# Row maxima by way of DRAM in 4-byte elements, in place of VectorE's transposition, in an attention block with a gated FFN

## The chip, the core and the metric

The kernel runs on one core of one Trainium2 chip. The metric is the device time of one execution in microseconds. The kernel before takes 1174.17 us (median of three runs, 1174.13 to 1174.26). Its engines are TensorE (PE, with its weight loads as PEld), VectorE (DVE), ScalarE (ACT), GpSimd (POOL) and SyncE (SP), which issues nearly all DMAs. Tiles lie in SBUF with 128 partitions; matmuls write to eight PSUM banks.

## What is computed

The reference is a pre-norm transformer block in float32 with one shared key and value head:

```
B, S, D, H, F = 1, 2048, 448, 16, 1792          # Dh = 28
q = (ln(x) @ wq) in 16 heads;  k = ln(x) @ wk;  v = ln(x) @ wv      # k, v: one head for all 16
p = softmax(q k^T * Dh ** -0.5)                                     # over 2048 keys
h = x + (p v, heads side by side) @ wo
out = h + (silu(ln(h) @ w1) * (ln(h) @ w3)) @ w2
```

## The kernel before

**Groups and steps.** The 2048 queries make four tiles of 512 (T), the 16 heads four sets of four. A group i, 0 to 15, is one tile of queries with four heads; head j of the group lies in partitions 32j to 32j + 27. Attention of a group runs over 16 steps, one for each 128 keys (`c`), so there are 256 steps. The loop takes them in pairs.

**Two passes over the scores.** The softmax subtracts each query's maximum before the exponential. The maxima of a group are found ahead, 20 steps before its heads: `Unit` multiplies 128 queries of one head with 512 keys into a PSUM bank (L277), and DVE takes the maximum over them into one column of MX (`red`, L283, or with a second half joined in, `both`, L291). The second pass (`Head`, L328) computes the scores the other way round, keys in the partitions and 512 queries along the row, as three matmuls of split high and low parts. ACT takes the exponential from PSUM (L338), and `pv` multiplies with the values (L346).

**How the maximum gets into the scores.** The 28 channels of a head leave four of its 32 partitions free. Partition 28 + 32j of the high plane of the group's query tile QS[i] holds the negated maximum of every query, and the key tile has a row of ones there. So the matmul of L328 subtracts the maximum. But `max_done` finds the maxima with queries in partitions: after L307, NEG[q, 4j + n] is the negated maximum of query 128n + q of head j. They have to get from 128 partitions with 16 columns into 4 partitions with 512 columns. Before, DVE's transposition of blocks of 32 x 32 (L308, into NGT) and four DMAs from SBUF to SBUF (`max_out`, L314), one for each 32 queries, do that.

**Order.** The order is written out by hand. ORDER gives, within a pair of steps, the place of each score unit (u, d, t), each head matmul (0a to 7c) and each `pv` (p). Everything else hangs on step numbers: `max_done(i)` at step 16i - 5 and `max_out(i)` at 16i - 4. Each is called at the end of its pair; the first head of group i comes early in the pair 16i. Instructions of an engine run in the order in which they are written, and each waits for its inputs. SP's instruction for a DMA takes its turn on SP, waits there, and then the transfer runs by itself; the DMAs have eight semaphores in rotation.

**Neighbours on SP.** Behind the maxima stand, in each group, four copies of the group before's softmax denominators (`sm<-OT`, L355), a write of their reciprocals to DRAM (`sd<-sm`, L363) and four reads that spread them over partitions (`rb<-sd`, L366). In group 2, gathers of queries (`QR<-QR`, L487 to L493) stand ahead of the maxima and behind them. Group 0's maxima are finished in a hand-written list (FRONT) ahead of the loop.

Of the kernel before, what the change touches and what calls it, by code (L numbers as in the profile page):

```python
# [8 lines left out]
F32 = mybir.dt.float32  # L9
# [13 lines left out]
T = 512  # L23
NT = S // T
NQ = T // P
# [25 lines left out]
def block_kernel(  # L51
# [13 lines left out]
    ve, se, ge, pe, sy = nc.vector, nc.scalar, nc.gpsimd, nc.tensor, nc.sync  # L65
# [4 lines left out]
    def f(ap):  # L70
        return ap.bitcast(F32)
# [6 lines left out]
    dr_pool = ctx.enter_context(tc.tile_pool(name="dr", bufs=2, space=DRAM))  # L78
# [5 lines left out]
    NEG = [keep.tile([P, 32], F32R, name="neg")] * 2  # L84
    NGT = [keep.tile([P, 32], F32, name=f"ngt{k}") for k in range(2)]
# [161 lines left out]
    QS, MX, PT, PO, WH, WS = {}, {}, {}, {}, {}, {}  # L247
# [56 lines left out]
    def max_done(i):  # L304

        neg = NEG[i % 2]
        ve.tensor_reduce(neg[:, :16], MX[i], axis=AX.X, op=ALU.max, negate=True)  # L307
        ve.transpose(NGT[i % 2], f(neg))  # L308

    def max_out(i):  # L310

        dst = f(QS[i][28::32, 0]).rearrange("j (n b x) -> j n b x", n=NQ, b=4)
        for b in range(4):
            sy.dma_start(dst[:, :, b], NGT[i % 2][32 * b : 32 * b + 16])  # L314
# [272 lines left out]
    def maxima(i):  # L587
        max_done(i)
        max_out(i)
# [29 lines left out]
    for i in range(1, NI):  # L619
        at(NC * i - 5, max_done, i)  # L620
        at(NC * i - 4, max_out, i)
# [218 lines left out]
```

## Time and profile before

| | before |
|---|---|
| median of the runs | 1174.17 us |
| the profiled execution | 1174.14 us |
| its span in the trace | 1172.0 us |
| attention with both passes | about 75 to 696 us of the span |
| FFN | from about 740 us to the end |
| PE, DVE, ACT, POOL busy | 99%, 69%, 62%, 29% |
| `max_done`: L307 and L308 | 16 times each, 0.22 and 0.21 us |
| `max_out`: L314 | 64 DMAs of 2 KB, on SP |

Times in the rows are us from the span's start. A timeline row gives start, length, engine, line, operation, tiles and shapes, how many were merged, and in brackets the idle time ahead and what ended it. A row of the windows gives the stretch, its length, the busy us of PE, PEld, DVE, ACT and POOL with their instructions, the granted share of TensorE's clock, the mean busy share of the 16 DMA engines and GB/s. A row of the waits gives who waited for whom, us in total, how often, and the longest.

### The profile page before, as it was taken

What the parts mean: (1) busy time and instruction counts of PE and PEld (TensorE: products, weight loads), DVE (VectorE), ACT (ScalarE), POOL (GpSimd) and SP (SyncE); (2) the same over time, 40 slices, a digit from 0 to 9 for tenths busy, and PEclk for the clock granted to TensorE, in tenths of its full rate; (3) what the DMA queues carried; (4) which work ended last, traced back from release to release, by engine and by line L of the source; (5) the groups of instructions that cost most, each with busy time, mean ns of one, the idle gap of its engine ahead of it and who ended that gap; (6) DMA issues with size and microseconds to landing.
All of it is one profiled execution on the core that took longest, in us unless ns stands there. A gap on an engine that the chain in (4) does not pass through costs nothing. (4 is left out here: it accounts for less than half of the span.)

```text
span 1172.0 us, 24130 instructions
## 1 busy us (share of the span) xinstructions
PE 1159.4 (99%) x9552; PEld 720.2 (61%) x9552; DVE 812.2 (69%) x1482; ACT 728.1 (62%) x1385; POOL 334.0 (29%) x275
## 2 busy tenths in 40 slices
PE   9999999999999999999999999999999999999998
PEld 7654444445444445444445443688888888888887
DVE  8879999997898997999987972364445445444443
ACT  5779999996899996999986999311211121111111
POOL 5202110110110111111011032364555445445552
PEclk9999999999999999999999999999999999999999
DMA  5110110000010000010000010113000000000000
GB/s 171 42 29 2 43 50 5 11 11 3 11 47 11 2 11 11 2 48 11 3 11 11 3 46 11 51 51 103 1 32 1 1 1 32 1 1 32 1 1 32
DMA packets 33158, 27.72 MB, mean 24 GB/s; under 512 B 11215, under 2 KB 29327, under 8 KB 33045
## 3 DMA queue, kind: packets, MB, share of 16 engines
q1 hardware_dynamic: 32484, 26.12, 7.6%
q8 instruction: 75, 1.23, 0.4%
q14 instruction: 39, 0.31, 0.1%
q10 hardware_dynamic: 560, 0.06, 0.0%
HBM read 20.25 MB, written 3.80 MB: 21 GB/s over the span
## 5 line engine op out<-in xcount | busy, mean ns | idle before, releaser
L338 ACT ACTIVATE pt<-pb 128x512 f32<-128x512 f32 x1024 | 531.7, 610 | 11.0 <-PE pb L328 5.2
L283 DVE TENSOR_REDUCE mx<-pa 128x1 f32<-128x512 f32 x708 | 460.9, 684 | 52.1 <-PE pb L328 36.9
L328 PE MATMUL pb<-qs,KH 32*128 32x512 f32 x2048 | 342.8, 431 | 0.1
L277 PE MATMUL pa<-KH,qs 32*128 32x512 f32 x866 | 327.4, 487 | 0.3
L346 PE MATMUL po<-pt,VA 128*32 128x256 f32 (+1 forms) x2984 | 298.1, 471 | 5.9 <-ACT OT L350 5.5
L328 PE MATMUL pb<-qs,KL 32*128 32x512 f32 x1024 | 283.2, 419 | 0.0
L328 PEld LDWEIGHTS pb<-qs,KH 32*128 32x128 f32 x2048 | 174.9, 182 | 114.1 <-DVE mx L283 50.0
L165 PE MATMUL pa<-xh,w 128*128 128x512 f32 x784 | 202.1, 391 | 0.0
L728 ACT ACTIVATE rb<-pa 128x512 f32<-128x512 f32 x56 | 30.4, 595 | 250.5 <-PE pa L720 250.4
L165 PEld LDWEIGHTS pa<-xh,w 128*128 128x128 f32 x784 | 146.1, 188 | 30.4 <-issue 1.2
L277 PEld LDWEIGHTS pa<-KH,qs 32*128 32x128 f32 x866 | 142.8, 181 | 9.5 <-issue 1.8
L328 PEld LDWEIGHTS pb<-qs,KL 32*128 32x128 f32 x1024 | 136.4, 182 | 2.4
L745 PE MATMUL pb<-w2s,hid 128*128 128x448 f32 x648 | 136.9, 366 | 0.0
L346 PEld LDWEIGHTS po<-pt,VA 128*32 128x32 f32 x2984 | 58.8, 108 | 122.7 <-issue 105.3
L745 PEld LDWEIGHTS pb<-w2s,hid 128*128 128x128 f32 x648 | 119.4, 188 | 17.3 <-issue 9.8
L287 ACT ACTIVATE relu<-pa 128x512 f32<-128x512 f32 x158 | 91.2, 600 | 58.7 <-PE pa L277 49.4
L392 POOL TENSOR_TENSOR w<-QR,w 128x1024 fp32r<-128x1024 f32 x32 | 84.0, 2641 | 94.2 <-PE pa L720 79.9
L291 DVE CUSTOM_DVE_ANT_0 relu<-pa,relu 128x512 f32<-128x512 f32 x158 | 105.5, 682 | 7.5 <-PE pa L277 4.1
L737 DVE TENSOR_TENSOR hid<-rb,hid 128x512 fp32r<-128x512 f32 x56 | 72.3, 1290 | 39.2 <-ACT hid L736 39.2
L370 POOL TENSOR_TENSOR OT<-OT,rb 128x512 f32<-128x512 f32 x16 | 20.5, 1284 | 273.5 <-ACT pt L338 147.0
L165 PE MATMUL pa<-xl,w 128*128 128x512 f32 x336 | 94.5, 389 | 0.0
L391 DVE CAST w<-QR 128x1024 fp32r<-128x1024 f32 x32 | 22.2, 695 | 89.5 <-PE pa L165 81.3
(125 smaller groups left out, 948.2 us busy)
## 6 DMA issues: line engine op xcount, KB each, us to landing
rb<-sd SPq DMA_DIRECT2D x64, 64.0 KB
QR<-in_B_w_dram SPq DMA_DIRECT2D x16, 192.0 KB
X<-in_A_x_dram SPq DMA_DIRECT2D x3, 896.0 KB
out_dram<-X SPq DMA_DIRECT2D x3, 896.0 KB
w<-in_B_w_dram SPq DMA_DIRECT2D x8, 192.0 KB
w_wo<-in_B_w_dram SPq DMA_DIRECT2D x6, 224.0 KB
qs<-ngt SPq DMA_DIRECT2D x64, 2.0 KB
sm<-OT SPq DMA_DIRECT2D x64, 2.0 KB
```

Of the source, the lines that this page charges most:

```text
L165: pe.matmul(ps, lhs[b][:, cb, lsl], rhs[a][:, ca, rsl], start=(k == 0), stop=(k == len(terms) - 1 and not part),)
L277: pe.matmul(self.ps, QS[i][r, 0, n * P : (n + 1) * P], ks[r], start=True, stop=True)
L283: ve.tensor_reduce(self.col(), self.ps, axis=AX.X, op=ALU.max)
L287: se.activation(r, self.ps, AF.Relu)
L291: ve.tensor_tensor_reduce(r, self.ps, r, 1.0, LOW, op0=ALU.add, op1=ALU.max, accum_out=self.col())
L328: pe.matmul(self.ps, (KH, KH, KL)[k][r, c * P : (c + 1) * P], QS[i][r, (0, 1, 0)[k]], start=(k == 0), stop=(k == 2))
L338: se.activation(pt, self.ps, AF.Exp, bias=0.0, scale=SCALE)
L346: pe.matmul(PO[i][32 * j : 32 * j + 32, q], VA[:, c], PT[i, c, j][:, q], start=(c == 0 and h0 == 0), stop=(c == NC - 1 and h1 == 2))
L392: ge.tensor_tensor(wl, W13[k], f(wh), op=ALU.subtract)
L728: se.activation(sg, ps[0], AF.Silu)
L737: ve.tensor_tensor(h[:, 1], sg, f(h[:, 0]), op=ALU.subtract)
L745: pe.matmul(Y[t][n][:, :D], hid[a][:, n * P : (n + 1) * P], w2s[:, b, :D], start=(k == 0 and m == 0), stop=(k == NF - 1 and m == 2))
```

## The change

For groups 1 to 15, `max_done` leaves the transposition out. `max_out` writes the 16 columns of NEG to a DRAM tile `mxd` of 4 x 512, where neighbouring columns of a partition lie 512 bytes apart and neighbouring partitions 4 bytes apart, so every run is one element of 4 bytes; there are 2048. A second DMA reads the four rows of 512 elements from DRAM into the four partitions of QS[i]. Group 0 keeps the transposition and the four DMAs.

```diff
         neg = NEG[i % 2]
         ve.tensor_reduce(neg[:, :16], MX[i], axis=AX.X, op=ALU.max, negate=True)
-        ve.transpose(NGT[i % 2], f(neg))
+        if i == 0:
+            ve.transpose(NGT[0], f(neg))
 
     def max_out(i):
 
+        if i > 0:
+            sd = dr_pool.tile([4, T], F32, name="mxd")
+            sy.dma_start(sd.rearrange("j (n q) -> q j n", n=NQ), f(NEG[i % 2][:, :16]).rearrange("q (j n) -> q j n", n=NQ))
+            sy.dma_start(f(QS[i][28::32, 0]), sd)
+            return
         dst = f(QS[i][28::32, 0]).rearrange("j (n b x) -> j n b x", n=NQ, b=4)
         for b in range(4):
             sy.dma_start(dst[:, :, b], NGT[i % 2][32 * b : 32 * b + 16])
```

The first place is DVE around the maxima of group 3, with what each instruction waits for. Before:

```order
L283 TENSOR_REDUCE mx_87<-pa 128x1 [waits PE_49] x6
L291 ISA relu,mx_87<-pa,relu 128x512 [waits PE_49]
L291 ISA mx_87 128x1
L307 TENSOR_REDUCE neg<-mx_87 128x16 [waits DVE_49]
L308 STREAM_TRANSPOSE ngt_84<-neg 128x32 [waits DMAHW2_49,DVE_49]
L283 TENSOR_REDUCE mx_86<-pa 128x1 [waits PE_49] x6
```

Now:

```order
L283 TENSOR_REDUCE mx_87<-pa 128x1 [waits PE_49] x6
L291 ISA relu,mx_87<-pa,relu 128x512 [waits PE_49]
L291 ISA mx_87 128x1
L307 TENSOR_REDUCE neg<-mx_87 128x16 [waits DMAHW0_49,DVE_49]
L283 TENSOR_REDUCE mx_86<-pa 128x1 [waits PE_49] x6
```

The transposition is gone, and the wait for the DMA of an earlier group that still may read the tile has moved from it to L307.

The second place is SP around the maxima of group 2, where gathers stand on both sides (the loop's L487 is L493 in the changed file). Before:

```order
L487 DMA QR_100<-QR_100 4x512 x2
L487 DMA QR_100<-QR_100 4x512 [waits DMAHW1_49]
L314 DMA qs<-ngt_83 4x4x32 [waits DVE_49,PE_49]
L314 DMA qs<-ngt_83 4x4x32
L314 DMA qs<-ngt_83 4x4x32 [waits DMAHW4_49]
L314 DMA qs<-ngt_83 4x4x32 [waits DMAHW5_49]
L487 DMA QR_100<-QR_100 4x512 [waits DMAHW6_49]
```

Now:

```order
L493 DMA QR_100<-QR_100 4x512 x2
L493 DMA QR_100<-QR_100 4x512 [waits DMAHW7_49]
L315 DMA mxd<-neg 128x16x1 [waits DVE_49]
L316 DMA qs<-mxd 4x512 [waits DMAHW0_49,PE_49]
L493 DMA QR_100<-QR_100 4x512 [waits DMAHW2_49]
```

Two DMAs stand in place of four, and the second waits on SP for the landing of the first (DMAHW0).

## The prediction

> **What bounds the kernel now.** I read the page first, then the windows of the attention stage, then VectorE's (DVE's) timeline around one place where the maxima of a group are finished, and last the DMA issues of SyncE.
>
> ```profile
> span 1172.0 us, 24130 instructions
> PE 1159.4 (99%) x9552; PEld 720.2 (61%) x9552; DVE 812.2 (69%) x1482; ACT 728.1 (62%) x1385; POOL 334.0 (29%) x275
> 317.00:400.00 83.00, 82.31 (x935) 37.80 (x932) 74.92 (x141) 78.72 (x152) 10.15 (x10) 1.00 0.08 21
> ```
>
> The 99% of PE tells little: matmul ends are modelled. In a stretch of pure attention (the third row: 83 us, then the busy us of PE, PEld, DVE, ACT, POOL) DVE is busy 90% and ACT 95%. PE, ACT and DVE run in lockstep, handing each other eight PSUM banks, so a delay on any of them that exceeds its slack lengthens the pair of steps in which it falls. The next fence is DVE's timeline. L291 runs once in each pair, so the distance between two L291 rows is a pair's length.
>
> ```profile
> 349.05 0.68 DVE L291 CUSTOM_DVE_ANT_0 relu<-pa,relu 128x512 f32<-128x512 f32 x1
> ...
> 353.93 0.68 DVE L291 CUSTOM_DVE_ANT_0 relu<-pa,relu 128x512 f32<-128x512 f32 x1
> 354.53 0.08 DVE L291 DVE_READ_ACCUMULATOR2_ANT mx<- 128x1 f32 x1
> 354.65 0.22 DVE L307 TENSOR_REDUCE neg<-mx 128x16 fp32r<-128x64 f32 x1
> 354.90 0.21 DVE L308 STREAM_TRANSPOSE ngt<-neg 128x32 f32<-128x32 f32 x1
> 355.04 3.12 DVE L283 TENSOR_REDUCE mx<-pa 128x1 f32<-128x512 f32 x5
> ...
> 359.15 0.68 DVE L291 CUSTOM_DVE_ANT_0 relu<-pa,relu 128x512 f32<-128x512 f32 x1
> ...
> 364.03 0.68 DVE L291 CUSTOM_DVE_ANT_0 relu<-pa,relu 128x512 f32<-128x512 f32 x1
> ...
> 374.42 0.68 DVE L291 CUSTOM_DVE_ANT_0 relu<-pa,relu 128x512 f32<-128x512 f32 x1
> ...
> 375.03 0.25 DVE L362 RECIPROCAL sm<-sm 128x16 f32<-128x16 f32 x1
> 375.19 1.82 DVE L283 TENSOR_REDUCE mx<-pa 128x1 f32<-128x512 f32 x3
> ...
> 379.30 0.68 DVE L291 CUSTOM_DVE_ANT_0 relu<-pa,relu 128x512 f32<-128x512 f32 x1
> ```
>
> An ordinary pair takes 353.93 - 349.05 = 4.88 us. The pair with the maxima takes 359.15 - 353.93 = 5.22, so 0.34 more, and the next is at 4.88 again. In an ordinary pair the reductions of L283 start with the accumulator read; here they start at 355.04 instead of 354.53, 0.51 late. The pair with the reciprocal has them only 375.19 - 375.03 = 0.16 late and takes 4.88: nothing lost. So DVE has between 0.16 and 0.51 us of slack in a pair, and what exceeds it is paid. The way it is paid shows on ScalarE:
>
> ```profile
> 356.94 3.21 ACT L338 ACTIVATE pt<-pb 128x512 f32<-128x512 f32 x6 [0.15 <-PE pb L328]
> PEld pb L328 <- DVE mx L283: 50.0, 123, 0.4
> ```
>
> The late reduction frees its bank late, PE starts the next scores late, and ACT waits 0.15 us for them in the middle of its exponentials.
>
> **The change, part by part.** First the transposition. It runs sixteen times, and fifteen of them go:
>
> ```profile
> L308 DVE STREAM_TRANSPOSE ngt<-neg x16: 211/211/213, 70.5 to 695.6; 128x32 f32<-128x32 f32 x16
> ```
>
> The fifteenth, at 695.6, has no reduction behind it (the score units are over), so removing it is worth nothing; fourteen count. What remains in front of the reductions is the reduction L307 and the gap before it. The transposition starts 0.25 after L307 (354.90 - 354.65), and that step goes out of the delay of 0.51: 0.26 remains. (A wait for the earlier copy of the maxima stands in front of L307 now; that copy is an entire group old, so only its few tens of ns could show.) What a delay of 0.26 costs is read from other rows. At the start of the attention DVE has casts at the same place:
>
> ```profile
> 93.81 0.68 DVE L291 CUSTOM_DVE_ANT_0 relu<-pa,relu 128x512 f32<-128x512 f32 x1
> ...
> 94.42 0.39 DVE L502 CAST WO<-OT 128x448 fp32r<-128x448 f32 x1
> 94.72 3.16 DVE L283 TENSOR_REDUCE mx<-pa 128x1 f32<-128x512 f32 x5
> ...
> 98.86 0.68 DVE L291 CUSTOM_DVE_ANT_0 relu<-pa,relu 128x512 f32<-128x512 f32 x1
> ...
> 103.91 0.68 DVE L291 CUSTOM_DVE_ANT_0 relu<-pa,relu 128x512 f32<-128x512 f32 x1
> 104.52 0.39 DVE L502 CAST WO<-OT 128x448 fp32r<-128x448 f32 x1
> ...
> 105.20 3.12 DVE L283 TENSOR_REDUCE mx<-pa 128x1 f32<-128x512 f32 x5
> ...
> 109.30 0.68 DVE L291 CUSTOM_DVE_ANT_0 relu<-pa,relu 128x512 f32<-128x512 f32 x1
> ```
>
> A delay of 0.30 (94.42 to 94.72) makes a pair of 5.05, 0.17 more; cast and maxima together, 0.68 late, make 5.39, 0.51 more. So the four points are 0.16: 0, 0.30: 0.17, 0.51: 0.34, 0.68: 0.51. Between the first two, 0.26 costs 0.17 x 0.10 / 0.14 = 0.12. A group saves 0.34 - 0.12 = 0.22. In group 1 the cast remains: 0.56 costs 0.39 by the last two points, so 0.51 - 0.39 = 0.12 is saved. Sum: 13 x 0.22 + 0.12 = **3.0 us**. Bounds: if the remaining 0.26 costs nothing, 13 x 0.34 + 0.39 = 4.8; if it costs as much as 0.30, 13 x 0.17 + 0.09 = 2.3.
>
> Second, the DMAs. SyncE issued four per group and issues two; it stands idle for most of a group, so the two saved issues are worth nothing. But the path is longer now: a write to DRAM of 2048 elements of 4 bytes, a wait for its landing, and a read back. The trace has such a chain, sd<-sm then rb<-sd, with 128 runs of 64 bytes in place of 2048 of 4:
>
> ```profile
> 375.31 0.35 SPq L363 DMA_DIRECT2D sd<-sm  x1
> 376.77 1.72 SPq L366 DMA_DIRECT2D rb<-sd  x4
> ...
> 246.05 1.70 SPq L366 DMA_DIRECT2D rb<-sd  x4
> 249.51 1.29 POOL L370 TENSOR_TENSOR OT<-OT,rb 128x512 f32<-128x512 f32 x1 [14.12 <-DMA rb<-sd]
> 376.00:376.20 0.20, 0.20 (x7) 0.15 (x8) 0.20 (x1) 0.20 (x2) 0.00 (x0) 1.00 0.14 14
> 376.20:376.40 0.20, 0.20 (x8) 0.01 (x2) 0.20 (x2) 0.20 (x2) 0.00 (x0) 1.00 0.32 27
> q1 hardware_dynamic: 32484, 26.12, 7.6%
> ```
>
> From the issue of the write to the issue that waits for it: 376.77 - 375.31 = 1.46. The read: the fourth issue of L366 begins about 246.05 + 1.70 - 0.42 = 247.3, and POOL, waiting for it, starts at 249.51: 2.2. The runs: the two windows hold a DMA share of 0.14 and 0.32, so (0.14 + 0.32) x 0.2 us x 16 engines = 1.5 us for 128 packets and 16 semaphore updates, 10.2 ns each. No row has 4-byte runs to DRAM. The lower bound of one is these 10.2 ns; the upper is the mean over all packets of SyncE's queue, 0.076 x 16 x 1172 / 32484 = 44 ns, at 804 bytes each. Spread over 16 engines, 2048 runs are 128 for each, 120 more than the row's 8. With p for one run, the chain takes 1.46 + 120p + 2.2 = 3.66 + 120p: **4.9 us** at 10.2 ns, 8.9 at 44. I take the lower end, since the 64-byte row is nearest in kind (short, SBUF to DRAM).
>
> What hides it is the distance to the first scores that use the row. Counted in order, the first head of group i is weight load 192i + 1 of L328:
>
> ```profile
> 149.37 2.29 SPq L314 DMA_DIRECT2D qs<-ngt  x4
> 154.68 0.18 PEld L328 LDWEIGHTS pb<-qs,KH 32*128 32x128 f32 x1
> 355.18 2.51 SPq L314 DMA_DIRECT2D qs<-ngt  x4
> 364.71 0.18 PEld L328 LDWEIGHTS pb<-qs,KH 32*128 32x128 f32 x1
> 695.35 0.22 DVE L307 TENSOR_REDUCE neg<-mx 128x16 fp32r<-128x64 f32 x1
> 702.39 0.19 PEld L328 LDWEIGHTS pb<-qs,KH 32*128 32x128 f32 x1
> ```
>
> In an ordinary group (7 here) L307 ends at 354.87, SP follows 0.07 after its releaser (355.11 to 355.18), so 364.71 - 354.94 = 9.8 us are there: hidden up to p = 51 ns. Group 15 has 702.39 - 695.64 = 6.75, up to 26 ns. Group 2 is the tightest: SP is busy issuing gathers until 149.37, so 5.3 us are there, and some 0.3 less once groups 1 and 2 are shorter: up to about 11 ns. At 10.2 nothing waits; at 44 group 2 waits 3.6 to 3.9 and group 15 2.2, together about 6. Groups 5, 9 and 13 lie in longer pairs and have more room. While SP waits for the write, what is queued behind it in group 2 is eight gathers and the denominators, all needed later; in the other groups nothing is queued for 13 us (355.18 to the denominators at 369).
>
> On the write a rule of the Trainium skill speaks against the change: "DMA: Bandwidth & Descriptors", Rules for kernel authors, says that a non-contiguous last dimension becomes one descriptor per element and should be rearranged. By that the count of 2048 is right, as I took it; the 64-byte rows agree with a cost by the packet, not by the byte.
>
> Sum: -3.0 for the pairs, 0 for the DMAs. The profiled execution took 1174.14 (span 1172.0), the median is 1174.17, so both give **1171.2 us**.
>
> **Rivals.** (1) Two groups wait. Between 11 and 51 ns a run, group 2 and, from 26, group 15 stop PE; at 44 ns this is 6 us against 3.0: 1177. At 25 ns it is 120 x 0.014 = 1.7: 1172.9. For it: 4 bytes go to DRAM in strides, which no row shows. Against it: the 10.2 ns of the 64-byte row. One page, "DMA: Bandwidth & Descriptors", Specifications, says that below 512 bytes the engine reads, modifies and writes; the 64-byte row shows no such cost, and no run so far has 4 bytes.
>
> (2) The rest of DVE's delay keeps its price. If the slack is nearer to 0.16 than the straight line has it, or the new wait lengthens the gap before L307, 0.30 and more remain late and only 2.3 or less is won: 1171.9 to 1172.8. For it: the price rises steeply just there.
>
> (3) Every group waits: the place is again the first head, the price begins at 51 ns a run. At 64 ns the chain takes 11.3 us: ten ordinary groups lose 1.5 each, group 2 6.0, group 15 4.6, so 26 - 3 = 23 more: 1197. For it: a 4-byte write may hold its DRAM line until the next, and neighbouring partitions write into the same line. Against it: even the mean packet of the queue takes 44.
>
> **How the numbers follow.** Forecast 0.46, (1) 0.27, (2) 0.14, (3) 0.13. From no change, a measurement of this kernel tells about 0.2%, 2.35 us. The forecast is beyond it for 0.43 of its 0.46; (1) gives 0.05 faster, 0.16 same, 0.06 slower; (2) is same with 0.13; (3) slower. Rounded: faster 0.49, same 0.32, slower 0.19. The forecast's own range is 1169.4 (all 4.8 won) to 1171.9. The range to 1177 takes in (1) and (2) and leaves out (3).
>
> **What would show it.** DVE's timeline: L307 directly before L283, the pair with maxima at about 5.00 instead of 5.22, ordinary pairs still 4.88. SP: from L315 to L316 about 2.7 us at 10.2 ns, 6.7 at 44; L316 is the direct measure of p. PEld: no wait for qs<-mxd in any group; a wait in group 2 alone means p between 11 and 26, in groups 2 and 15 up to 51. The FFN stage (from 740 us) must keep its 432 us. The prediction is wrong if the pairs stay at 5.22 without the transposition, or if L316 comes later than 5.5 us after L315.

## The result, and the profile after

The changed kernel takes 1230.49 us (median of four runs, 1229.72 to 1232.34) beside 1174.15 for the kernel before: a ratio of 1.0481, 95% interval 1.0469 to 1.0493. It is 56.3 us slower; the forecast was 3.0 faster. The profiled execution took 1229.72, with a span of 1227.9. From its page:

```profile
span 1227.9 us, 24051 instructions
PE 1184.0 (96%) x9552; PEld 726.9 (59%) x9552; DVE 812.2 (66%) x1467; ACT 731.6 (60%) x1385; POOL 333.6 (27%) x275
PEclk9999989999988999998989988999999999999999
```

PE's busy share has fallen from 99% to 96%, and in many slices of the attention stage the granted clock is no longer whole. The forecast called the distance from L315 to L316 the direct measure. SP's timeline in group 3 (start, length, line, tiles):

```profile
197.98 0.37 SPq L315 DMA_DIRECT2D mxd<-neg  x1
208.30 0.54 SPq L316 DMA_DIRECT2D qs<-mxd  x1
```

That is 10.32 us where 2.7 was forecast. The view of the waits says whom SP waits for (us in total, times, longest):

```profile
SPq L316 <- DMA mxd<-neg: 128.8, 13, 10.3
PE pb L334 <- DMA qs<-mxd: 31.0, 10, 7.4
```

It is the landing of the write: in all 15 groups L316 comes 10.0 to 10.8 us behind L315 (the view names the wait in 13). At the end of the chain PE waits for the read (L334 is the head matmul, L328 before; for some groups the trace puts PE's wait down to another name, so the 31.0 is not all of it). What the DMA engines do in these 10 us shows in the windows of the same group (stretch, length, busy us of PE, PEld, DVE, ACT, POOL, granted clock, DMA share, GB/s):

```profile
198.00:201.00 3.00, 3.00 (x42) 1.49 (x40) 2.96 (x5) 2.76 (x7) 0.00 (x0) 1.00 0.34 8
201.00:208.30 7.30, 7.07 (x75) 2.92 (x71) 5.89 (x13) 6.52 (x13) 1.06 (x2) 1.00 0.00 0
```

The packets are gone after 3 us: 0.34 x 3.0 us x 16 engines over 2048 elements and 16 semaphore updates is 7.9 ns each, less than the 10.2 of the forecast. Then the engines stand idle for 7.3 us, and only after that has the write landed. PE's timeline at the end of the chain:

```profile
207.57 0.50 PE L277 MATMUL pa<-kd,qs 32*128 32x512 f32 x1
210.25 0.47 PE L334 MATMUL pb<-qs,KH 32*128 32x512 f32 x1 [2.18 <-DMA qs<-mxd]
```

The read took 210.25 - 208.30 = 1.95 us to the first head (2.2 forecast), and PE stood for 2.18.

DVE's side came out as forecast; its timeline in the same group:

```profile
197.01 0.68 DVE L291 CUSTOM_DVE_ANT_0 relu<-pa,relu 128x512 f32<-128x512 f32 x1
197.74 0.22 DVE L307 TENSOR_REDUCE neg<-mx 128x16 fp32r<-128x64 f32 x1
197.87 3.20 DVE L283 TENSOR_REDUCE mx<-pa 128x1 f32<-128x512 f32 x5
...
202.01 0.68 DVE L291 CUSTOM_DVE_ANT_0 relu<-pa,relu 128x512 f32<-128x512 f32 x1
```

The pair is 202.01 - 197.01 = 5.00 long, as predicted, 5.22 before.

**A second loss.** Around most of PE's waits the clock is halved. Three windows around the first head of group 7, and then one each at the heads of groups 3 and 6:

```profile
389.00:390.30 1.30, 0.00 (x0) 0.00 (x0) 1.25 (x4) 1.22 (x3) 0.96 (x2) 1.00 0.03 6
390.30:397.20 6.90, 6.18 (x45) 2.98 (x47) 3.52 (x8) 4.28 (x9) 0.92 (x1) 0.51 0.00 0
397.20:399.00 1.80, 1.80 (x22) 0.63 (x19) 1.80 (x4) 1.58 (x3) 0.00 (x0) 1.00 0.03 2
...
210.00:240.00 30.00, 29.40 (x339) 13.70 (x339) 26.31 (x49) 27.68 (x54) 3.19 (x3) 1.00 0.05 11
...
346.00:378.50 32.50, 31.94 (x336) 14.49 (x336) 26.44 (x48) 28.18 (x55) 3.51 (x4) 0.90 0.15 43
```

PE is empty (0.00), then the granted clock is 0.51 for 6.9 us, then whole again. Behind group 3's wait the clock stayed at 1.00 and 339 matmuls took 30.0 us; group 6 has 0.90 over 32.5 us for 336. Counted over the trace there are ten such stretches of 0.5, each of 3.41, 6.83 or 10.24 us, 61.4 us together, one at the first head of every group that waited except 3 and 8. The last section shows what sets these two apart.

To see the two losses apart, each group is cut at two rows: from the end of L307 to the group's first head ("chain", where PE's wait lies), and from that head to the end of the next L307, for the last group to the start of the FFN stage ("rest", where the half clock lies). Sums over the groups, in us:

| | chain | rest | half clock at the heads |
|---|---|---|---|
| before | 164.5 | 504.5 | none |
| changed | 202.6 | 523.0 | in ten groups |
| 64-byte runs (experiment 2) | 162.0 | 504.6 | none |

The FFN stage is the same in all of them within 0.3 us. Against a kernel whose chain is short, the change loses 40.6 us in waits and 18.4 in the clock.

### The profile page after: what moved, and what is told of

Same layout as the page of the kernel before. It is cut to its first block, busy times and chain, and to the rows that moved or that the text cites. A ratio compares the mean times of both kernels' runs of the same rounds, so it can differ in the third digit from the quotient of the medians.

```text
span 1227.9 us, 24051 instructions
## 1 busy us (share of the span) xinstructions
PE 1184.0 (96%) x9552; PEld 726.9 (59%) x9552; DVE 812.2 (66%) x1467; ACT 731.6 (60%) x1385; POOL 333.6 (27%) x275
## 5 line engine op out<-in xcount | busy, mean ns | idle before, releaser
L334 PE MATMUL pb<-qs,KH 32*128 32x512 f32 x2048 | 350.9, 448 | 35.8 <-DMA qs<-mxd 31.0
L277 PE MATMUL pa<-KH,qs 32*128 32x512 f32 x866 | 332.5, 498 | 0.3
L352 PE MATMUL po<-pt,VA 128*32 128x256 f32 (+1 forms) x2984 | 306.6, 483 | 2.3 <-ACT OT L356 1.9
L334 PE MATMUL pb<-qs,KL 32*128 32x512 f32 x1024 | 292.0, 432 | 0.0
L334 PEld LDWEIGHTS pb<-qs,KH 32*128 32x128 f32 x2048 | 177.8, 191 | 160.4 <-DVE mx L283 68.5
L334 PEld LDWEIGHTS pb<-qs,KL 32*128 32x128 f32 x1024 | 139.6, 191 | 3.4
```

The costliest lines, as they stand in the source:

```text
L277: pe.matmul(self.ps, QS[i][r, 0, n * P : (n + 1) * P], ks[r], start=True, stop=True)
L334: pe.matmul(self.ps, (KH, KH, KL)[k][r, c * P : (c + 1) * P], QS[i][r, (0, 1, 0)[k]], start=(k == 0), stop=(k == 2))
L352: pe.matmul(PO[i][32 * j : 32 * j + 32, q], VA[:, c], PT[i, c, j][:, q], start=(c == 0 and h0 == 0), stop=(c == NC - 1 and h1 == 2))
```

## The experiments

**1. What a write costs, by its form.** The kernel before, with one unused write of the maxima to DRAM added at the end of `max_out` in each of the groups 3 to 14, and a read that waits for it; nothing uses the result. The diff shows the forms of groups 3 and 4. The price is the time from the write's issue to the issue of the read.

```diff
+        probe(i)
+
+    def probe(i):
+        if not 3 <= i <= 14:
+            return
+        src = f(NEG[i % 2][:, :16])
+        pd = dr_pool.tile([2048, 16], F32, name="pd")
+        flat = pd.rearrange("a b -> (a b)")
+        out, part = flat[:2048], src
+        at0 = 1024 if i == 13 else 0
+        if i == 3:
+            out, part = out.rearrange("(e q) -> q e", e=16), src
+        elif i == 4:
+            out, part = pd.rearrange("(e q) b -> q e b", e=16)[:, :, 0], src
...
+        sy.dma_start(out, part)
...
+            sy.dma_start(PSINK[:1, :1], flat[at0 : at0 + 1].rearrange("(a b) -> a b", b=1))
```

> The kernel before (transposition kept), with one extra write that nothing of the computation uses behind the maxima of each of the groups 3 to 14, and behind it a read of one written element that waits for the landing; so the time from the issue of the write to the issue of that read is the price of the write alone. In the changed kernel this took 10.2 us for 2048 runs of 4 bytes, although all packets had left by about 2.5 us. Theory M (each short write to DRAM costs about 4.5 ns in the memory, one after another, whatever the engines do): group 3, the same pattern: 10.2; group 4, every element 64 bytes from the next: about 10; group 5, the 16 elements of a partition within 128 bytes: about 10; group 6, the same 2048 elements into SBUF: about 3; group 7, half the elements: 5.8; group 8, 1024 runs of 8 bytes: 5.8; group 9, 512 runs of 16 bytes: 3.5; group 10, 128 runs of 64 bytes: 1.5; group 12, elements 32 bytes apart: 10; group 13, two writes of 1024: 10; group 14, 64 partitions: 5.8. Rival L (writes of neighbours to one line of DRAM wait for each other): groups 4 and 12 fall to about 3, group 5 stays at 10 or rises. Rival D (making 2048 descriptors is what takes the time): group 6 also takes about 10. Group 11 reads 2048 elements of 4 bytes from DRAM: about 3 by M and L, 10 by D. The time of the kernel stays within 0.5% of before by all.

SP's timeline: the change's form, the same elements 64 bytes apart, the same form into SBUF, and 64-byte runs.

```profile
187.11 0.44 SPq L353 DMA_DIRECT2D pd<-neg  x1
197.30 0.25 SPq L357 DMA_DIRECT2D psink<-pd  x1
...
227.61 0.45 SPq L353 DMA_DIRECT2D pd<-neg  x1
231.92 0.23 SPq L357 DMA_DIRECT2D psink<-pd  x1
...
318.40 0.70 SPq L353 DMA_DIRECT2D psink<-neg  x1
321.36 0.65 SPq L355 DMA_DIRECT2D psink<-psink  x1
...
489.25 0.44 SPq L353 DMA_DIRECT2D pd<-neg  x1
490.86 0.23 SPq L357 DMA_DIRECT2D psink<-pd  x1
```

| what is written | us |
|---|---|
| 2048 elements of 4 bytes, neighbours in DRAM (the change's form) | 10.19 |
| half the columns of it, 1024 elements | 10.19 |
| 64 of its partitions, 1024 elements | 9.73 |
| in two writes of 1024, behind each other | 11.03 |
| a partition's 16 elements side by side, 8 bytes apart | 10.16 |
| 2048 elements 32 bytes apart | 4.41 |
| 2048 elements 64 bytes apart | 4.31 |
| 2048 elements, neighbours, into SBUF | 2.96 |
| 1024 runs of 8 bytes | 4.38 |
| 512 runs of 16 bytes | 2.23 |
| 128 runs of 64 bytes | 1.61 |
| for comparison: 2048 elements of 4 bytes read from DRAM | 2.68 |

The price isn't the number of elements: half of them cost the same, and all of them 64 bytes apart cost 4.31. Nor is it what the engines do for each run, since into SBUF the same runs take 2.96. It arises where small writes lie close together in DRAM. So theory M is out (5.8 for half the elements, 10 for those 64 bytes apart), and rival D with it (10 into SBUF). Rival L has the closeness right, but had about 3 for elements that lie apart. The kernel took 1174.6 with these writes (one run): by themselves they disturb nothing.

**2. 64-byte runs.** The changed kernel, with each partition's 16 values written as one run. The queries' order in the row is another one then, so a query gets the maximum of another query or head subtracted. The softmax divides such a constant out, but for rounding; that no exponential gets an argument above zero is no longer assured.

```diff
-            sy.dma_start(sd.rearrange("j (n q) -> q j n", n=NQ), f(NEG[i % 2][:, :16]).rearrange("q (j n) -> q j n", n=NQ))
+            sy.dma_start(sd.rearrange("j m -> (j m)").rearrange("(e q r) -> q e r", q=P, r=16), f(NEG[i % 2][:, :16]).rearrange("q (e r) -> q e r", r=16))
```

> The changed kernel, with the 16 maxima of a partition written to DRAM as one run of 64 bytes (128 runs), so that the row read back holds the maxima in another order. The softmax divides by a sum with the same shift, so the order does not change what is computed but for rounding. Theory W (the price of the change is the wait for the slow write, with what follows from it): write to read 1.5 us, the first head of a group waits for nothing, pairs with maxima 5.00 us, no half clock: 1171.2 us, 0.25% faster than before. Rival T (leaving the transposition out is worth nothing, or the DMAs disturb others): 1174 us or more.

1171.16 us (1170.67 to 1171.83), ratio 0.9976 (0.9966 to 0.9986). SP's timeline in group 7:

```profile
353.99 0.35 SPq L315 DMA_DIRECT2D mxd<-neg  x1
355.73 0.54 SPq L316 DMA_DIRECT2D qs<-mxd  x1
```

and DVE's:

```profile
353.01 0.68 DVE L291 CUSTOM_DVE_ANT_0 relu<-pa,relu 128x512 f32<-128x512 f32 x1
...
358.02 0.68 DVE L291 CUSTOM_DVE_ANT_0 relu<-pa,relu 128x512 f32<-128x512 f32 x1
```

The landing takes 1.74, the pair 5.01, and no ordinary group waits: the way over DRAM without the transposition is worth the 3.0 us of the forecast, where the runs are longer. So the whole loss, 59.3 us between the two kernels, hangs on the form of one write.

**3. 8-byte runs.** The same with r=2 in both rearrangements, 1024 runs; the order is another one again.

```diff
-            sy.dma_start(sd.rearrange("j m -> (j m)").rearrange("(e q r) -> q e r", q=P, r=16), f(NEG[i % 2][:, :16]).rearrange("q (e r) -> q e r", r=16))
+            sy.dma_start(sd.rearrange("j m -> (j m)").rearrange("(e q r) -> q e r", q=P, r=2), f(NEG[i % 2][:, :16]).rearrange("q (e r) -> q e r", r=2))
```

> The changed kernel with runs of 8 bytes, 1024 of them, the row in another order as above. Theory M, 4.5 ns per run in the memory: write to read about 5.8 us, ready 7.8 us after the issue, so ordinary groups (9.8 us) wait for nothing, group 2 waits about 2.5 us and group 15 about 1; with at most two stretches of half clock behind those: 1174 to 1181 us. Rival B (the price goes by bytes or by lines, not by runs): write to read stays at about 10 us and the time stays near 1230 us.

1171.98 us (1171.45 to 1173.93), ratio 0.9986 (0.9977 to 0.9995). SP in group 7, then PE in group 2, then the window behind that head:

```profile
355.43 0.37 SPq L315 DMA_DIRECT2D mxd<-neg  x1
359.84 0.53 SPq L316 DMA_DIRECT2D qs<-mxd  x1
...
156.17 0.47 PE L334 MATMUL pb<-qs,KH 32*128 32x512 f32 x1 [1.26 <-DMA qs<-mxd]
...
156.00:186.00 30.00, 29.48 (x339) 13.82 (x342) 26.38 (x50) 27.77 (x54) 3.18 (x3) 1.00 0.19 49
```

A landing of 4.41 is hidden everywhere but in group 2, as the forecast's slacks have it (chain 4.4 + 2.0 = 6.4 against 5.0 there). Group 2's wait of 1.26 is followed by no half clock. Both expectations missed the landing: theory M had 5.8, and with it a wait in group 15 too, and rival B about 10.

**4. The transposition kept, and moved.** The kernel before, with L308 and its four DMAs one pair later than L307, so that DVE's delay is shared by two pairs.

```diff
-        ve.transpose(NGT[i % 2], f(neg))
+    def max_turn(i):
+        ve.transpose(NGT[i % 2], f(NEG[i % 2]))
...
-        at(NC * i - 4, max_out, i)
+        at(NC * i - (5 if i == NI - 1 else 3), max_turn, i)
+        at(NC * i - (4 if i == NI - 1 else 3), max_out, i)
```

> The kernel before, with the transposition kept but one pair of steps later than the reduction that finds the maxima (groups 1 to 14), so that no pair has both. If the price of a delay of DVE in a pair is as read (0.16 us free, 0.26 costs 0.12, 0.51 costs 0.34), the pair with L307 takes 5.00 and the pair with the transposition 4.88 to 4.95: 14 times 0.15 to 0.22 is won, 1171 to 1172 us. If the two delays cost the same apart as together, 1174.2 us.

1170.56 us (1170.24 to 1171.38), ratio 0.9971 (0.9959 to 0.9982). DVE's timeline (the transposition is L311 here):

```profile
352.11 0.68 DVE L291 CUSTOM_DVE_ANT_0 relu<-pa,relu 128x512 f32<-128x512 f32 x1
352.83 0.22 DVE L307 TENSOR_REDUCE neg<-mx 128x16 fp32r<-128x64 f32 x1
...
357.11 0.68 DVE L291 CUSTOM_DVE_ANT_0 relu<-pa,relu 128x512 f32<-128x512 f32 x1
357.71 0.21 DVE L311 STREAM_TRANSPOSE ngt<-neg 128x32 f32<-128x32 f32 x1
357.84 1.84 DVE L283 TENSOR_REDUCE mx<-pa 128x1 f32<-128x512 f32 x3
...
361.98 0.68 DVE L291 CUSTOM_DVE_ANT_0 relu<-pa,relu 128x512 f32<-128x512 f32 x1
```

Pairs of 5.00 and 4.87: the transposition alone makes the reductions 0.13 late (357.84 - 357.71) and costs nothing, within the slack of at least 0.16 that the forecast read. All that removing it could win is to be had by moving it, with no DRAM. This version is faster than both kernels. From the 64-byte runs its interval doesn't tell it apart; the 0.6 between them lies in the chain sums (161.4 and 162.0), of which group 2 has 9.62 and 10.17.

**5. How wide is the neighbourhood?** As experiment 1, other forms, all with 4-byte elements.

```diff
+            3: (128, 16, 2, False), 4: (128, 16, 4, False), 5: (128, 2, 1, False), 6: (128, 1, 1, False),
+            7: (32, 16, 1, False), 8: (16, 16, 1, False), 9: (8, 16, 1, False), 10: (4, 16, 1, False),
+            11: (2, 16, 1, False), 12: (128, 16, 4, True), 13: (128, 4, 2, True), 14: (16, 16, 16, False),
```

The four entries are partitions, columns, the distance in elements, and whether a partition's elements are the neighbours.

> Probes as in the first set, all with runs of 4 bytes, again one behind each of the groups 3 to 14, read as the time from the issue of the write to the issue of the read behind it. The first set: 2048 elements in the pattern of the change 10.2 us; half of its columns 10.2; 64 of its partitions 9.7; elements 32 or 64 bytes apart 4.4 and 4.3; runs of 8 bytes 4.4, of 16 bytes 2.2, of 64 bytes 1.6; into SBUF 3.0. So the count does not set it. Theory L (writes into the same 64 bytes of DRAM are served one after another, some 0.55 to 0.6 us each; lines go side by side): group 5 (2 columns, 256 elements) and group 6 (1 column, 128 elements) still about 10; group 7 (32 partitions) and group 8 (16 partitions, one line per column) 9 to 10; group 9 (8 partitions, 8 writes per line) about 5; group 10 (4) about 2.5; group 11 (2) 1.6; group 14 (16 partitions, each element its own line) 1.6; group 3 (8 bytes apart) about 5; group 4 (16 apart) about 4.4; groups 12 (partition by partition, 16 bytes apart) 4.4 and 13 (4 elements of each partition, 8 bytes apart) 2.5. Rival G (the memory serves a larger region, some hundred bytes, one write after another, so the density of writes in it counts): groups 5 and 6 still about 10, group 8 about 2.5 and group 9 below 2. Rival N (number of writes in all): group 5 about 2.5, group 6 about 1.9, group 8 2.5.

| written | us |
|---|---|
| 2048 elements, neighbours 8 / 16 bytes apart | 7.61 / 5.74 |
| 2 columns / 1 column of 128 neighbours (256 / 128 elements) | 7.63 / 7.18 |
| 16 columns of 32 / 16 / 8 / 4 / 2 neighbours | 5.77 / 3.08 / 1.56 / 1.65 / 1.46 |
| 16 columns of 16, 64 bytes apart (256 elements) | 3.62 |
| a partition's 16 elements side by side, 16 bytes apart | 7.75 |
| a partition's 4 elements side by side, 8 bytes apart | 2.53 |

SP's timeline: one column of 128 neighbours, then 16 columns of 16, then of 8.

```profile
318.01 0.44 SPq L333 DMA_DIRECT2D pd<-neg  x1
325.19 0.23 SPq L334 DMA_DIRECT2D psink<-pd  x1
...
397.85 0.45 SPq L333 DMA_DIRECT2D pd<-neg  x1
400.93 0.23 SPq L334 DMA_DIRECT2D psink<-pd  x1
...
437.67 0.47 SPq L333 DMA_DIRECT2D pd<-neg  x1
439.23 0.22 SPq L334 DMA_DIRECT2D psink<-pd  x1
```

128 elements of one column cost 7.18, nearly as much as 2048 in 16 columns; 256 elements in columns of 16 cost 3.08. So the price goes largely with the number of neighbours that follow each other, and columns go on at the same time. If each 64 bytes were held by themselves, columns of 16 neighbours would cost as much as those of 128; they don't, so theory L is out, and so is rival N (1.9 for one column). Less the 1.5 of a write that pays nothing, columns of 16 neighbours (64 bytes) pay 1.6 us, of 32 4.3, of 64 8.2 (experiment 1) and of 128 (the change's form) 8.7: some 0.10 to 0.13 a neighbour up to 64, and little more beyond. That would fit a region of about 256 bytes in which small writes go one by one, as rival G has it. It doesn't fit all rows: G had about 10 for one and for two columns; 16 elements of a column 64 bytes apart, four in 256 bytes, take 3.62, more than the same elements side by side (3.08) and than columns of 4 (1.65); and 16 neighbours of one partition, 8 or 16 bytes apart, are as dear or dearer (10.16, 7.75) than neighbours of 16 partitions at the same distance (7.61, 5.74). The width of the region and what happens in it stay open.

**6. Taking the half clock away.** The changed kernel, with transpositions of the identity on PE ahead of each first head that waits (24, and 64 and 48 in groups 2 and 15), into a PSUM bank that nothing reads.

```diff
+        if s % NC == j == k == 0 and s // NC in FILL:
+            w = bank()
+            for _ in range(FILL[s // NC]):
+                pe.transpose(w[:, :P], ident, ident)
+            done(w)
```

> The changed kernel, with transpositions of the identity (work that nothing uses, about 0.11 us each) on PE ahead of the first head of a group, where PE otherwise stands idle: 24 in ordinary groups, 64 in group 2, 48 in group 15. Of the 59 us between the changed kernel and the one with runs of 64 bytes, the waits of the first heads are 40 us (27.5 in ten ordinary groups, 7.4 in group 2, 5.6 in group 15) and 19 us are left. Theory C (those 19 us are TensorE at half clock, which is granted for some us behind an idle stretch): with PE kept at work through the wait, the rows show no half clock, or little, and the time is about 1212 us. Rival R (the rest is engines that have to fall into step again, or the half clock has another cause): 1228 us or more, since the filling saves nothing and may cost.

1230.15 us (1229.55 to 1231.28), ratio 1.0479 (1.0461 to 1.0496): nothing won, and the expectation was missed. The mean granted clock rose from 0.974 to 0.997 and the rest-sum fell by 10.8 us to 512.2, but the filler was too long, so that the heads of ordinary groups came 0.2 to 1.9 us later than in the changed kernel, and in group 15 it stood behind the waiting head, since there the head with j = 1 is the first. Another 2.2 us were lost at the start of the FFN stage (425.4 us in place of 423.2). PE's timeline in group 15:

```profile
747.68 0.76 PE L334 MATMUL pb<-qs,KH 32*128 32x512 f32 x1 [5.13 <-DMA qs<-mxd]
...
750.67 7.05 PE L665 MATMUL pb<-ident 128*128 128x128 f32 x48
```

**7. The same, mended.** 16 transpositions, 56 in group 2 and 40 in group 15, there ahead of the head with j = 1.

> The filling again, mended: in the last group the first head is that of lane 1, so that the 48 transpositions stood behind the waiting head and made the stage 8 us longer; and in the ordinary groups 24 were too many, the heads came 0.5 to 2 us after the row was there. Now 16 in ordinary groups, 56 in group 2, 40 in group 15, all ahead of the first head. Theory C (half clock behind an idle PE costs 18 us): the first heads wait as in the changed kernel (40 us in all), the stretches from a first head to the next maxima take 29.9 us in every ordinary group, no half clock: 1230.5 - 18.4 + 0 to 4 us = 1212 to 1216 us. Rival R (the filling can't win anything): 1228 us or more.

1214.55 us (1213.15 to 1215.41), ratio 1.0340 (1.0321 to 1.0358). The granted clock is 1.000 throughout, the rest-sum 504.4, that of the kernel before. PE's timeline in group 3:

```profile
205.58 1.97 PE L665 MATMUL pb<-ident 128*128 128x128 f32 x16
...
207.81 0.47 PE L334 MATMUL pb<-qs,KH 32*128 32x512 f32 x1 [0.27 <-DMA qs<-mxd]
```

PE fills the wait instead of standing, the head comes no earlier (the chain-sum is 206.3, 3.7 above the changed kernel's), and 15.9 us are won. So the half clock was the second cost, 18.6 us in the rest-sum, and PE's idleness brought it about.

**8. Elements 32 bytes apart in DRAM.** The changed kernel with a DRAM tile eight times as large; the read is strided then.

```diff
-            sd = dr_pool.tile([4, T], F32, name="mxd")
-            sy.dma_start(sd.rearrange("j (n q) -> q j n", n=NQ), f(NEG[i % 2][:, :16]).rearrange("q (j n) -> q j n", n=NQ))
-            sy.dma_start(f(QS[i][28::32, 0]), sd)
+            sd = dr_pool.tile([4 * T, 8], F32, name="mxd")[:, 0]
+            sy.dma_start(sd.rearrange("(j n q) -> q j n", j=4, n=NQ), f(NEG[i % 2][:, :16]).rearrange("q (j n) -> q j n", n=NQ))
+            sy.dma_start(f(QS[i][28::32, 0]), sd.rearrange("(j m) -> j m", j=4))
```

> The changed kernel with each element of 4 bytes in DRAM 32 bytes from the next, so that the same 2048 short writes no longer share lines, and a read back of 4 rows of 512 elements, each its own run. Theory L: the write takes 4.4 us instead of 10.2; the read is 512 runs for each of the 4 engines that serve 4 partitions, at 10 ns 5.1 us and some 1.5, so the row is there about 11 us after the issue: ordinary groups wait 1 to 1.5 us, group 2 about 6, group 15 about 4: 1171 + 20 to 25, 1191 to 1196 us, and more if half clock follows waits as short as these. Theories by the count of runs: write 10.2, and the whole slower than the changed kernel, 1270 us or more.

1211.11 us (1210.41 to 1214.83), ratio 1.0320 (1.0303 to 1.0337), worse than expected. SP in group 3, then PE:

```profile
195.96 0.37 SPq L315 DMA_DIRECT2D mxd<-neg  x1
200.44 0.58 SPq L316 DMA_DIRECT2D qs<-mxd  x1
...
207.53 0.46 PE L334 MATMUL pb<-qs,KH 32*128 32x512 f32 x1 [1.49 <-DMA qs<-mxd]
```

The write landed in 4.48, as experiment 1 had it, with as many elements and packets as the change has. But the read, 4 partitions with 512 elements of 4 bytes each, took 7.1 us in place of 1.95: most of what was won on the way out (5.8 us) was lost on the way in (5.1). Beside the 64-byte runs, about 33 us go in waits and 6.5 in the clock, with six stretches of half clock. The trace has 2048 packets of 4 bytes more for it than the changed kernel's group.

## Why the prediction was wrong

**The pairs: right.** "Removing it" was worth 3.0 us by the forecast's sum. The pairs went from 5.22 to 5.00, the others stayed at 4.88, and with a write that lands early the kernel took 1171.16 beside the forecast's 1171.2. The price table read from casts at the same place (0.26 late costs 0.12) held, and so did its lower end: 0.13 late costs nothing (experiment 4). One small term was off. In group 1 the forecast left 0.56 of delay, but 0.68 less the 0.25 of the transposition is 0.43; in experiment 2 that pair takes 5.18, so that 0.21 is saved, not 0.12. Rival (2) is out.

**The step that failed** is the term of the write, "I take the lower end, since the 64-byte row is nearest in kind". The p of 10.2 ns was the time that a packet occupies a DMA engine, and as that it was about right (7.9 ns here). The chain, however, waits for the landing, and of that the row said nothing: its 128 runs of 64 bytes have no neighbours of 4 bytes, so its 1.46 us held no such cost. Measured from L315 to L316, p is (10.32 - 1.46) / 120 = 74 ns, above even the upper bound of 44, which was a mean over packets' engine time too; and the 10.32 us lie past the 5.5 that the prediction had named as a sign of being wrong. Nor is it a price per run: half the runs land no earlier (10.19, experiment 1), so the form 120p failed along with its size. Nearest in kind meant nearest in size and direction; what decided was where the neighbours' bytes go. No row could tell that; the honest bound from above was open.

On this the Trainium skill had a line that the forecast didn't weigh: "DMA: Bandwidth & Descriptors", in Anatomy of one DMA — SWDGE (gpsimd) path, puts most of a DMA's fixed cost down to the receipt of the last byte in the target memory and calls that cost about constant, 2.0 us. The section is on DMAs that GpSimd issues, and this write is issued by SP. The place agrees with the 7.3 us in which the engines were idle; a constant doesn't, with 1.5 to 10.3 us between forms of one write.

**The hidden chain: right but for p.** With 74 ns, put in to stand for the landing, the forecast's own formula, 3.66 + 120p, gives 12.5 us: ten ordinary groups lose 2.7 each, group 2 7.5, group 15 5.8, together 40.3. Measured: 40.6. The slacks of 9.8, 5.0 and 6.75 and the read were right to a few tenths, and groups 5, 9 and 13 did not wait. Between 1171.16 and experiment 7's 1214.55, the kernel without the half clock, lie 43.4, of which 3.7 are the filler's.

**Rival (3)** named the place, the cause in kind (neighbouring partitions writing close together; its single line is not shown, see experiment 5) and the point where it begins; it was underpriced, at 1197 for 64 ns. Its argument against itself, "even the mean packet of the queue takes 44", is the same error of reading engine time for landing. Rival (1)'s pattern appeared with 8-byte runs, where group 2 alone waited.

**What no case held** is the clock: 18.4 of the 59.3 us. The forecast took a wait of PE to cost its own length. Here a wait of 2.1 to 2.5 us cost in eight of ten ordinary groups another 1.0 to 1.3, or 2.1 to 2.2 us, behind it (rest 31.0 to 31.2, or 32.0 to 32.4, for 29.9 to 30.2).

**The DMAs on SP: right.** The two issues saved per group were worth nothing, and nothing was queued behind the waiting L316 that somebody missed: the rest-sum of experiment 7, where SP waits as long, is that of before.

## What to carry to other kernels

The time that packets occupy DMA engines is not the time until a write has landed: read the price of a write from its issue to the first instruction that waits for it, and take it from a write of the same pattern in the target memory, not of the same packet size. Where values must be scattered through DRAM, make the runs as long as the layout lets you, and look whether the reader's arithmetic tolerates another order, as the softmax's does here but for the bound on its exponents. A small operation that overruns an engine's slack may only need to be moved to the next pair, and a wait that empties PE may cost more than its length.

## What the runs showed of the hardware

**Small writes into neighbouring bytes of DRAM.** 2048 elements of 4 bytes land in 10.2 us, in 4.3 when 64 bytes apart, in 3.0 in SBUF, and the same 8 KB in 1.6 as runs of 64 bytes; 128 elements in a row take 7.2.

**PE's clock.** In the ten ordinary groups that waited (2.14 to 2.50 us), eight heads met 3.41 or 6.83 us at half the granted clock, and two none (groups 3 and 8, 2.18 and 2.33 us). What decides is where the wait lies. The stretches of half clock last multiples of 3.41 us, and within a run they start whole multiples of 3.413 us apart, so the clock goes by units of that length which don't begin with the wait. In the attention stage of the ten traces, each of the 17 units at whole clock in which PE stood 1.38 us or more was followed by half clock, and none with 1.37 or less was; the half clock ended behind the first unit in which PE did not stand. (In the FFN stage of experiment 6 a unit with 1.65 was followed by no half clock, so this bound is one of attention.) Two waits of experiment 8, in its units:

```profile
114.55:117.96 3.41, 2.03 (x27) 0.92 (x23) 1.60 (x5) 1.47 (x3) 1.16 (x1) 1.00 0.01 0
117.96:121.38 3.42, 3.42 (x31) 1.87 (x29) 1.72 (x3) 2.90 (x6) 0.00 (x0) 0.50 0.02 5
...
380.79:384.20 3.41, 2.22 (x19) 0.75 (x19) 2.13 (x5) 2.69 (x6) 1.88 (x2) 1.00 0.25 1
384.20:387.62 3.42, 2.12 (x29) 1.32 (x29) 1.37 (x3) 1.08 (x2) 0.00 (x0) 1.00 0.00 0
387.62:391.03 3.41, 3.05 (x37) 1.17 (x33) 3.11 (x6) 3.39 (x7) 0.00 (x0) 1.00 0.00 0
```

Group 1's wait of 1.38 us lies in one unit (3.41 - 2.03), and the next has 0.50. Group 7's wait of 2.49 is split into 1.19 and 1.30, and the clock stays whole. Groups 3 and 8 of the changed kernel are split so too (1.36 and 0.82, 1.20 and 1.13). "TensorE: Matmul & The Clock Gate" of the Trainium skill, HAM oscillation, gives idle gaps over about 3.4 us as what brings the clock down. The unit of 3.4 agrees with the trace; the gap doesn't, since 1.38 us within one unit sufficed.

**Many short reads into few partitions.** 2048 elements of 4 bytes, read into 4 partitions, took 7.1 us (experiment 8, 32 bytes apart in DRAM); in experiment 1 as many, side by side and read into 128, took 2.68. No run separates the number of partitions from the distance.
